# Parameter stage rebuilt: the left rows of x first, the matrices' angles by TensorE, 21 projection groups there, and table rounds without matrices

## The chip, the cores and the metric

The kernel runs on one core of a Trainium2 chip. The metric is the time of one execution on the device in microseconds (us), the median of three runs. The engines are TensorE (PE in the profile, with its weight loads as PEld), VectorE (DVE), ScalarE (ACT), GpSimd (POOL) and SyncE (SP, which only issues transfers here).

## The reference

Two independent parts, `a` (a recurrent attention with a memory) and `b` (an S4 convolution), cut to what is computed:

```python
def _A_ref(x, mem0, Wq, Wk, Wv, Wo, seg_len):     # x (1,2048,1024), 32 heads of 128, memory 8 rows, segments of 32
    for s in range(n_seg):                        # 64 segments, each needs the memory that the one before left
        h = concatenate([mem, x[:, s*32:(s+1)*32]])
        q, k, v = h @ Wq, h @ Wk, h @ Wv
        p = softmax(where(mask, q k^T * scale, -1e9))
        o = (p v) @ Wo
        mem = o[:, :8]; outs.append(o[:, 8:])

def _B_ref(u, A_re, A_im, B_re, B_im, C_re, C_im, log_dt, Dskip):    # u (1,2048,1024), 128 states a channel
    dt = exp(log_dt); logdA = dt * (A_re + 1j*A_im); dB = dt * (B_re + 1j*B_im)
    P = exp(logdA[:, :, None] * arange(2048))
    K = einsum('dn,dnl,dn->dl', C_re + 1j*C_im, P, dB).real
    y = irfft(rfft(u, 4096) * rfft(K, 4096))[:2048] + u * Dskip      # convolution along time
```

## The kernel before, in words

There are four stages, one behind the other, since each needs what the one before it made.

**Parameter stage** (0 to about 101 us). The matrices A, B, C of part b, 128 partitions by 1024 values each, are turned into modulus, angle and turn of each state (`modulus`, `turn`, `angle`), and each result is cut into two or three bf16 parts (`put3`) that are stored to `PB` in DRAM. `matrices` fills `MF`, the cosines and sines of the Fourier matrices in bf16: per pair of columns VectorE makes the angles (L774), ScalarE rounds (L776), VectorE subtracts (L769) and takes the absolute (L765), ScalarE takes two sines (L766, L770). `transposes` loads x in 16 blocks of 128 rows (L98), transposes each by 8 matmuls (L108), and ScalarE keeps the last 8 of each 32 rows in `xTl` and sends the other 24 to `VXd` in DRAM (L111, L112). These last 8 rows of a segment are called the left rows here: their keys, queries and values can be projected ahead of the recurrence. `projections` does that, in groups of 8 matmuls of 512 columns (L168); 10 groups run in this stage. A loop steps the generators in turn.

**Table rounds** (to about 415 us). Sixteen rounds make the powers P from the parts. The order of one round is the string `ORDER`, whose words stand in program order on each engine; a dash marks work of the round before. `X?p` are the two power matmuls of an e (L1131) into the PSUM tile `pa`, of which there is one; `E?` is the exponential of 648 columns that ScalarE takes from it (L1139); `X?t` is the phase matmul (L1125) and `n?` VectorE's copy of it; `S?` and `C?` are sines and cosines of 1824 columns on ScalarE, `b?` an absolute on VectorE, `gi?` and `gr?` its products, `K?` the matmuls that sum them. Exponentials and sines need different function tables, so each round holds two ACT_TABLE_LOADs, one at the first exponential (L1139) and one at the first sine (L1152). Between this stand side jobs: `P` a projection group (six a round), `U` a group of the spectra of u (L961), and `M` eight transposes of `MF` (L940), copied by VectorE and stored to `MId` in DRAM by GpSimd. The words `p?`, `A?`, `u?` and `m` copy the results of the side jobs out of PSUM. Each sine also issues one of 15 copies of 512 KB from weights (12 of them DRAM to DRAM), and the evictions of projections issue queued stores, among them 16 value rows `VXd<-PVd` of 256 KB.

**Pointwise stage** (b = 0 to 15, to about 655 us). For each b, `spectrum(b)` is 64 matmuls of 256 columns (L1101), `pointwise(b)` is ten VectorE operations of 1024 columns (L1265 to L1276), which write `Bt`. From b=4, two `inverse` groups of 32 matmuls each (L1324) follow each spectrum; they read `MI`, the transposed matrices, which SyncE loads from `MId` at b=0 to 3. spectrum(b+1) stands ahead of pointwise(b) in program order.

**Attention** (to the end). 64 segments, one after the other; TensorE works on the projections and waits for weights `wst` that are streamed from the copies `WD` in DRAM.

Of the kernel before, what the change touches and what calls it, by code (L numbers as in the profile page):

```python
# [74 lines left out]
class Ahead:  # L75
# [18 lines left out]
    def transposes(self, pool, ps, ident):  # L94
        nc = self.nc
        def load(b):
            xb = pool.tile([128, self.Dm], BF16, name="xb", tag="xb")
            nc.gpsimd.dma_start(out=xb[:], in_=self.x[b * 128:(b + 1) * 128, :])  # L98
            return xb
        xbs = [load(b) for b in range(3)]  # L100
        yield
        for b in range(self.S // 128):
            if b + 3 < self.S // 128:
                xbs.append(load(b + 3))
            xb = xbs[b]
            pt = ps.tile([128, self.KC, 4, self.SL], BF16, name="pt_x", tag="ptx")
            for kc in range(self.KC):
                nc.tensor.transpose(out=pt[:, kc, :, :].rearrange("p a b -> p (a b)"), in_=xb[:, kc * 128:(kc + 1) * 128], identity=ident[:])  # L108
            yield
            xst = pool.tile([128, 4, self.KC, self.XM], BF16, name="xst", tag="xst")  # L110
            nc.scalar.copy(out=xst[:].rearrange("p s k r -> p k s r"), in_=pt[:, :, :, 0:self.XM])  # L111
            nc.scalar.copy(out=self.xTl[:, :, 4 * b:4 * b + 4, :], in_=pt[:, :, :, self.XM:self.SL])  # L112
            nc.sync.dma_start(out=self.VXd[4 * b:4 * b + 4, :, 256:].rearrange("s p f -> p s f"), in_=xst[:].rearrange("p s k r -> p s (k r)"))
            yield

    def projections(self):
# [3 lines left out]
        slices = [(m, t, c) for m, t, cs in (("k", 0, (0, 8)), ("v", 0, (0, 4)), ("q", 0, (0, 8)), ("v", 0, (4, 8)), ("k", 1, (0, 8)), ("v", 1, (0, 4)),  # L120
                                             ("q", 1, (0, 8)), ("v", 1, (4, 8))) for c in range(*cs)]

        def load(i):
            m, t, c = slices[i]
            w = self.pool.tile([128, KC, 256], BF16, name="wsl", tag="wsl", bufs=4)
            nc.sync.dma_start(out=w[:], in_=self.src(m)[:, :, 2048 * t + 256 * c:2048 * t + 256 * c + 256].rearrange("k p f -> p k f"))
            return w
        ws = [load(0), load(1), load(2)]
        take, vals = yield
        late = []  # L130
# [1431 lines left out]
```

## Time and profile before

| what | value |
|---|---|
| median of 3 runs | 2026.26 us (2025.77 to 2030.95) |
| the profiled execution | 2021.33 us, its span 2019.6 us |
| busy: PE, PEld, DVE, ACT, POOL | 1835.2, 1154.4, 1437.1, 949.2, 440.1 us |
| parameter stage (windows 0 to 102): PE, DVE, ACT, POOL busy | 39.3, 84.9, 69.4, 19.1 us |
| Sin load of the first round, of the last round | 113.24, 414.87 us |
| first operation of pointwise(0) (L1265) | 429.87 us |
| spectrum(5) starts | 477.79 us |

All times below are of the profiled execution, counted from the start of its span. The profile gives the busy time of every engine in 40 slices of the span; the timeline of an engine lists its instructions in order of start, with the idle time just before one and what ended it in brackets; a windows row gives the busy time of each engine in a stretch, then the granted TensorE clock, the share of time that the 16 DMA engines were busy, and what they moved. The busy time of a matmul is modelled and can overlap its neighbour, so steps are read from start to start.

### The profile page before, as it was taken

How to read it: one execution, taken by the hardware profiler on the slowest of the kernel's cores; microseconds unless marked ns; L12 is line 12 of the kernel's file. 1: busy time of each engine (PE TensorE's matmuls, PEld its weight loads, DVE VectorE, ACT ScalarE, POOL GpSimd, SP SyncE). 2: the span in 40 equal slices, each digit the busy share in tenths (PEclk: the TensorE clock that was granted, in tenths of full speed). 3: DMA queues.
4: the chain of work that ended last, by engine and by line, in shares of the span. 5: the costliest groups of instructions: out<-in, count | busy, mean ns of one | idle time of the engine just before them, and what ended most of it. 6: DMA issues, size and time to landing. Idle time of an engine off the chain costs nothing.

```text
span 2019.6 us, 75101 instructions
## 1 busy us (share of the span) xinstructions
PE 1835.2 (91%) x32170; PEld 1154.4 (57%) x32198; DVE 1437.1 (71%) x3442; ACT 949.2 (47%) x1662; POOL 440.1 (22%) x864
## 2 busy tenths in 40 slices
PE   1699999778999789999999999999999999999998
PEld 1365766567888445555555555555555555555554
DVE  8879999999998356766667666666766666676650
ACT  4888898831333334344444434344444434344430
POOL 2135555547000011111111111111111111111120
PEclk9999999998999889999999999999999999999999
DMA  6788996868456999999999999999999999999991
GB/s 172 187 231 270 265 269 179 221 188 264 153 158 231 343 326 348 339 336 345 345 345 350 332 335 353 344 335 344 351 324 343 346 344 352 336 349 332 345 346 40
DMA packets 352630, 591.60 MB, mean 293 GB/s; under 512 B 111312, under 2 KB 229408, under 8 KB 350248
## 3 DMA queue, kind: packets, MB, share of 16 engines
q1 hardware_dynamic: 297452, 527.25, 77.2%
q10 hardware_dynamic: 44812, 28.26, 4.6%
q0 software_dynamic: 10032, 31.28, 4.4%
q8 instruction: 252, 4.13, 0.8%
q14 instruction: 82, 0.67, 0.1%
HBM read 531.12 MB, written 66.05 MB: 296 GB/s over the span
## 4 chain that ended last, share of the span: by engine, by line
PE 37%; DMA 23%; DVE 4%; issue 1%; ACT 1%; POOL 0%; SPq 0%; ACTq 0%; DVEq 0%; POOLq 0%
PE acc L375 21%; DMA wst<-WD_v 9%; PE pp L488 8%; DMA wst<-WD_o 7%; PE pe L625 3%; DMA wst<-WD_k 2%; PE tr L386 2%; DMA wst<-WD_q 2%; DMA arena<-PKd 2%; PE pv L460 1%; PE pv L456 1%; DVE arena L582 1%; PE sc L400 1%; DVE arena L441 1%; ACT arena L582 1%
## 5 line engine op out<-in xcount | busy, mean ns | idle before, releaser
L375 PEld LDWEIGHTS <-a_hT 128*32 128x32 bf16 x12352 | 326.4, 96 | 320.0 <-issue 60.9
L381 ACT CAST arena<-acc 128x512 bf16<-128x512 f32 x384 | 224.7, 585 | 396.2 <-PE acc L375 320.8
L375 PE MATMUL acc<-W,a_hT 128*32 128x512 bf16 x4608 | 354.1, 381 | 0.0
L488 PEld LDWEIGHTS <-arena 128*32 128x32 bf16 x8256 | 217.2, 97 | 86.8 <-issue 63.4
L375 PE MATMUL acc<-wst,a_hT 128*32 128x512 bf16 x2304 | 229.6, 382 | 29.3 <-DMA wst<-WD_v 22.0
L389 POOL COPY arena<-arena 128x128 bf16<-128x128 bf16 x128 | 37.4, 292 | 840.7 <-DMA arena<-PKd 315.6
L296 DVE TENSOR_SCALAR arena<-keep 128x256 int32<-128x256 int32 (+1 forms) x512 | 175.4, 394 | 29.5 <-PE acc L375 28.3
L375 PE MATMUL acc<-MF,a_hT 128*32 128x512 bf16 x2048 | 172.0, 382 | 0.0
L488 PE MATMUL pp<-W_o,arena 128*32 128x256 bf16 x4096 | 138.2, 275 | 5.0 <-DMA W_o<-in_A_Wo_dram 5.0
L168 PE MATMUL pro<-xTl,wsl 128*128 128x512 bf16 x490 | 113.0, 383 | 12.5 <-ACT xTl L112 6.6
L415 DVE TENSOR_REDUCE a_mx<-sc 128x4 f32<-128x160 f32 (+1 forms) x192 | 71.6, 373 | 73.6 <-PE sc L403 71.8
L419 ACT ACTIVATE sc<-sc 128x160 f32<-128x160 f32 (+1 forms) x192 | 63.9, 333 | 122.6 <-DVE sc L416 121.9
L1101 PEld LDWEIGHTS <-MF 128*128 128x128 bf16 x1024 | 102.5, 100 | 30.8 <-issue 8.2
L503 DVE COPY arena<-tr 128x512 bf16<-128x512 bf16 x64 | 27.2, 425 | 126.7 <-PE tr L386 126.7
L423 DVE TENSOR_REDUCE a_mx<-sc 128x4 f32<-128x160 f32 (+1 forms) x192 | 72.8, 379 | 55.3 <-ACT sc L419 54.9
L1101 PE MATMUL hps<-KT,MF 128*128 128x256 bf16 x720 | 94.2, 283 | 15.0 <-DVE x L1266 11.1
L1139 ACT ACTIVATE E<-pa 128x648 bf16<-128x648 f32 x128 | 90.9, 710 | 33.1 <-PE pa L1131 27.9
L1324 PE MATMUL yp<-Bt,MI 128*128 128x256 bf16 x680 | 102.8, 273 | 0.7 <-ACT yb L1339 0.7
L450 POOL TENSOR_TENSOR arena<-arena,a_BD 128x128 bf16<-128x128 bf16 x128 | 51.1, 399 | 234.0 <-DVE arena L433 221.5
L582 ACT CAST arena<-pp 128x128 bf16<-128x128 f32 x64 | 17.0, 265 | 163.2 <-DVE arena L582 163.2
L168 PEld LDWEIGHTS <-wsl 128*128 128x128 bf16 x512 | 50.5, 99 | 72.0 <-issue 16.2
L375 PE MATMUL acc<-W_v,a_hT 128*32 128x512 bf16 x1280 | 91.1, 378 | 0.0
(330 smaller groups left out, 3892.1 us busy)
## 6 DMA issues: line engine op xcount, KB each, us to landing
wst<-WD_v SPq DMA_DIRECT2D x256, 512.0 KB
wst<-WD_k SPq DMA_DIRECT2D x192, 512.0 KB
wst<-WD_o SPq DMA_DIRECT2D x192, 512.0 KB
wst<-WD_q SPq DMA_DIRECT2D x128, 512.0 KB
Ud<-ux POOLq DMA_DIRECT2D x16, 1024.0 KB, 5.9
uq<-Ud SPq DMA_DIRECT2D x32, 512.0 KB
wsl<-in_A_Wk_dram SPq DMA_DIRECT2D x16, 512.0 KB
wsl<-in_A_Wv_dram SPq DMA_DIRECT2D x16, 512.0 KB
```

The lines of the kernel that those rows point to most:

```text
L168: nc.tensor.matmul(a[:], lhsT=w[:, kc, 128 * j:128 * j + 128], rhs=xTl[:, kc, :, :].rearrange("p s k -> p (s k)"), start=(kc == 0), stop=( ...
L296: nc.vector.tensor_scalar(out=out.bitcast(I32), in0=in_.bitcast(I32), scalar1=0, scalar2=None, op0=ALU.bitwise_or)
L375: nc.tensor.matmul(a[32 * g:32 * g + 32, o_:o_ + rhs.shape[1]], lhsT=hT[:, kc, :], rhs=rhs, start=(kc == 0), stop=(kc == KC - 1), tile_pos ...
L381: nc.scalar.copy(out=q, in_=a[:])
L415: nc.vector.tensor_reduce(out=m_, in_=x, axis=AX.X, op=ALU.max)
L419: nc.scalar.activation(out=flat(sc, i), in_=flat(sc, i), func=ACT.Exp, scale=scale)
L423: nc.vector.tensor_reduce(out=m_, in_=x, axis=AX.X, op=ALU.add)
L488: nc.tensor.matmul(po[32 * qt:32 * qt + 32, o_:o_ + rhs.shape[1]], lhsT=oT[:, h % 4, (h % 16) // 4, :], rhs=rhs, start=False, stop=(h == 3 ...
L625: nc.tensor.matmul(pe[n][:], lhsT=left[2 * b + hi // 16][:, 128 * (hi % 16):128 * (hi % 16) + 128], rhs=wo[u][:, 1024 * hh + 512 * n:1024 ...
L1101: pe.matmul(s_[r][half][:, cs, :], lhsT=MF[:, kc, 4 * rr + mc, cs, :], rhs=rhs, start=(i == 0 and mc == 0), stop=(i == 1 and mc == 3), ski ...
L1139: sc.activation(out=T["E", r, e // 4][:, lo:lo + 8 * NE].rearrange("p (i c) -> p i c", i=2), in_=T.pop(("p", r, e))[:, :, 0:4 * NE], func= ...
L1324: pe.matmul(yp[:, b, :], lhsT=m_[:, b, cs, kc, :], rhs=Bt[:, kc, j, half, c_, :], start=(kc == 0 and cs == 0 and half == 0), stop=(kc == 3 ...
```

## The change

- **Left rows first.** Only the left rows of x are loaded in the parameter stage: four loads of 128 rows, 8 transposes each, four copies into `xTl`. The other 24 rows of each segment go through `other_rows` in the pointwise stage: 16 blocks of 96 rows, 8 transposes and a ScalarE copy each, 3 blocks at b=2, 7 at b=3 and 6 at the start of b=4. Two blocks share one tile; two such tiles are loaded at first, and the next pair is loaded when the second block of a pair is transposed.
- **Angles by TensorE.** `matrices` goes. Seven small rows on each side give the angle of every element of `MF` as a matmul with 7 contracted rows (32 matmuls of 128x512, words `F`), and ScalarE takes one sine of each from 16 bits of the PSUM values (words `f`). 24 small transposes and three copies prepare the rows.
- **Parameter algebra.** The reciprocal and the minimum and maximum are replaced by logarithm and exponential on ScalarE and some products on GpSimd; the loads are split between the queues of SyncE and ScalarE; the order of the whole stage is written out by hand in `PAR`.
- **Projections.** 21 groups run in the parameter stage (10 before), and five a round (six before). Weight slices are 512 columns wide in two tiles, and a group of the values is 8 matmuls of 512 columns (16 of 256 before).
- **Rounds.** No `M` and no trip through `MId`; a new `ORDER`; the exponential of an e is two instructions of 324 columns, one for each bank of `exps`.
- **Moved to the pointwise stage.** `matrices_back` at b=0, 1 and 2 (5, 6 and 5 times 8 transposes), copied by ScalarE straight into `MI`. The 15 copies and the 16 value rows are issued two and two a b from b=4.

```diff
-    def transposes(self, pool, ps, ident):
...
+    def other_rows(self, two, stage, bank, ident):
+        nc, n = self.nc, 4 * self.XM
+        x_s = self.x.rearrange("(s r) d -> s r d", r=self.SL)
+        blocks = list(range(self.NS // 4))
+        xbs = []
+
+        def load():
+            t_ = two()
+            for i in range(2):
+                b = blocks.pop(0)
+                xb = t_[0:n, 1024 * i:1024 * i + 1024]
+                nc.gpsimd.dma_start(out=xb, in_=x_s[4 * b:4 * b + 4, 0:self.XM, :])
+                xbs.append((b, xb))
+        load()
+        load()
         yield
+        while xbs:
+            b, xb = xbs.pop(0)
+            pt = bank()[:, :, 0:n]
             for kc in range(KC):
+                nc.tensor.transpose(out=pt[:, kc, :], in_=xb[:, 128 * kc:128 * kc + 128], identity=ident[0:n, 0:n])
+            xst = stage()
+            nc.scalar.copy(out=xst.rearrange("p s k r -> p k s r"), in_=pt.rearrange("p k (s r) -> p k s r", r=self.XM))
+            nc.sync.dma_start(out=self.VXd[4 * b:4 * b + 4, :, 256:].rearrange("s p f -> p s f"), in_=xst.rearrange("p s k r -> p s (k r)"))
+            if b % 2 and blocks:
+                load()
             yield
...
+        def matrix(i):
+            mt = take([128, 512], F32, "mf")
+            pe.matmul(mt[:], lhsT=turns_l[:, i // 2, :], rhs=turns_r[:, i % 2, :], start=True, stop=True)
+
+            def evict():
+                sc.activation(out=MF[:, :, i // 2, i % 2, :], in_=mt[:].bitcast(I16)[:, 0:1024:2].rearrange("p (k n) -> p k n", k=4), func=ACT.Sin,
+                              scale=float(TWO_PI / 65536))
+            return evict
...
+    exps = ps_e.tile([128, 2, 512], F32, name="pa", tag="pa")
...
     def power_matmuls(r, e):
         r, e = (r, e) if e else (r + 1, 0)
-        pa = T["p", r, e] = ps_e.tile([128, 2, 512], F32, name="pa", tag="pa")
         for i in range(2):
-            pe.matmul(pa[:, i, 0:4 * NE], lhsT=pars[r][:, e, :], rhs=RE[:, 4 * i:4 * i + 4, :].rearrange("p a b -> p (a b)"), start=True, stop=True)
+            pe.matmul(exps[:, i, 0:4 * NE], lhsT=pars[r][:, e, :], rhs=RE[:, 4 * i:4 * i + 4, :].rearrange("p a b -> p (a b)"), start=True, stop=True)
...
-        sc.activation(out=T["E", r, e // 4][:, lo:lo + 8 * NE].rearrange("p (i c) -> p i c", i=2), in_=T.pop(("p", r, e))[:, :, 0:4 * NE], func=ACT.Exp)
+        for i in range(2):
+            sc.activation(out=T["E", r, e // 4][:, lo + 4 * NE * i:lo + 4 * NE * i + 4 * NE], in_=exps[:, i, 0:4 * NE], func=ACT.Exp)
...
+    def matrices_back(n):
+        for _ in range(n):
+            c = turned_back.pop(0)
+            mt = ps_m.tile([128, 2, 4, 128], BF16, name="mt", tag="m")
+            for kc in range(4):
+                for cs in range(2):
+                    pe.transpose(out=mt[:, cs, kc, :], in_=MF[:, kc, c, cs, :], identity=ident[:])
+            sc.copy(out=MI[c // 2][:, c % 2], in_=mt[:])
...
+    held = bp.tile([128, 4, 2, 2, 2, DQ], BF16, name="xst", tag="B")[:].rearrange("p a b c d e -> p (a b c d e)")
...
     for b in range(16):
         dq = b // 4
+        if b == 4:
+            for _ in others:
+                pass
...
+        matrices_back((5, 6, 5)[b] if b < 3 else 0)
+        for _ in range({2: 3, 3: 7}.get(b, 0)):
+            next(others)
...
-        if b < 4:
-            for i in (2 * b, 2 * b + 1):
-                sy.dma_start(out=MI[i][:], in_=MId[2 * i:2 * i + 2].rearrange("c p a k q -> p c a k q"))
+        for _ in range(2 if b >= 4 else 0):
+            for jobs in (copies, ahead.after):
+                if jobs:
+                    jobs.pop(0)()
```

## The prediction

> **What bounds the kernel now.** I read the slices of the page first, then the timelines of ScalarE, TensorE and VectorE at the points where one stage hands over to the next, then busy time by windows. The two rows of slices below cut the span into 40 parts of 50.5 us.
>
> ```profile
> PE   1699999778999789999999999999999999999998
> ACT  4888898831333334344444434344444434344430
> ```
>
> Slices 1 and 2 (to 101 us) are the parameter stage, slices 3 to 9 the table rounds, 10 to 13 the pointwise stage, the rest attention. TensorE is idle only in the parameter stage and around the hand-over at 400 to 475. Attention is not touched. The rounds come next, as ScalarE ran one of them (start, duration, instruction, idle time before and releaser):
>
> ```profile
> 201.94 1.28 ACT L1139 ACT_TABLE_LOAD   x1 [0.40 <-DVE gr L1114]
> 203.24 0.71 ACT L1139 ACTIVATE E<-pa 128x648 bf16<-128x648 f32 x1
> 203.84 0.58 ACT L177 CAST kst<-pro 128x512 bf16<-128x512 f32 x1
> 204.47 0.71 ACT L1139 ACTIVATE E<-pa 128x648 bf16<-128x648 f32 x1
> ...
> 211.01 0.71 ACT L1139 ACTIVATE E<-pa 128x648 bf16<-128x648 f32 x1 [0.63 <-PE pa L1131]
> 212.25 0.71 ACT L1139 ACTIVATE E<-pa 128x648 bf16<-128x648 f32 x1 [0.53 <-PE pa L1131]
> 212.97 1.28 ACT L1152 ACT_TABLE_LOAD   x1
> ```
>
> The Sin load returns every 19.95 us: 11.03 from the Exp load to the Sin load, 8.9 from there to the next Exp load, which waits for VectorE's last product. In the 11.03, one exponential starts per 1.24 to 1.34 us: `pa` is one buffer, an exponential is .71, and the refill by two matmuls costs the .53 of the last rows. TensorE is nearly full there too (19.89 of 20 us), so either could set the period. The round of 381.47 tells: only two of its six projection groups are left and TensorE works 13.35 of 20 us, yet it lasts 19.95 to the next Exp load, as the others do.
>
> ```profile
> 381.47 1.28 ACT L1139 ACT_TABLE_LOAD   x1 [0.40 <-DVE gr L1114]
> 401.43 1.28 ACT L1139 ACT_TABLE_LOAD   x1 [0.87 <-DVE gr L1114]
> 414.87 1.28 ACT L1152 ACT_TABLE_LOAD   x1
> ```
>
> So the rounds are bound by the ring of ScalarE, `pa` and VectorE, and a projection group taken out of them frees nothing. Then TensorE at the hand-over to the second half of the pointwise stage:
>
> ```profile
> 468.28 6.62 PE L1101 MATMUL hps<-KT,MF 128*128 128x256 bf16 x36 [4.84 <-DVE x L1266]
> ...
> 477.79 4.09 PE L1101 MATMUL hps<-KT,MF 128*128 128x256 bf16 x36
> ...
> 484.78 7.15 PE L1324 MATMUL yp<-Bt,MI 128*128 128x256 bf16 x64
> 491.77 4.09 PE L1101 MATMUL hps<-KT,MF 128*128 128x256 bf16 x36
> ```
>
> spectrum(5) starts right behind spectrum(4); from there one b is 128 matmuls in 13.98 us (477.79 to 491.77), back to back; the windows show how little is spare (length, then busy time of PE, PEld, DVE, ACT and POOL, clock, DMA share, GB/s):
>
> ```profile
> 494.00:508.00 14.00, 14.00 (x131) 12.55 (x129) 13.21 (x15) 5.17 (x7) 11.47 (x19) 1.00 0.52 154
> 508.00:522.00 14.00, 14.00 (x130) 12.54 (x129) 13.25 (x15) 6.39 (x8) 0.57 (x2) 1.00 0.65 210
> ```
>
> **Parameter stage: -36.** It ends, before, with an Exp load at 100.59 and the first Sin load at 113.24. The matrices' work leaves VectorE: 16 scalings at .44 from start to start, 8 subtractions at 1.14 and 8 absolutes at .6 are 21 us. A reciprocal of 6.55 goes too. ScalarE loses 8 magnitude copies at 1.04 and 16 sines at 1.05 (25 us), and the 16 copies of x of .7 (11 us); it gets 32 sines of 128x512. Their nearest rows are the 512-wide copies, .48 to .56, so 17 us. Summed from such rows, ScalarE has 54 us of work after (8 table loads 10, sines 17, copies of parts 10, other activations 8, copies of left rows, transposed columns and projections 7, issues 2), VectorE 49, GpSimd 20. TensorE has 21 projection groups at 1.87 (39 us) and 32 small matmuls at about .24 (8 us). It can start the groups when parameters, left rows and the first slice are in: 3.5 MB at the 243 GB/s of the first 20 us is 14.4. Then it ends at 61.5 and is the last; an eviction and a table load follow, and the first exponential is at 63.5 if nothing waits on anything else. Before, the longest engine, VectorE, was busy 84.9 of 102 us. With all of that waste the first exponential would be near 75. I take 66, nearer the sum since an order written out by hand interleaves the four engines; bounds 60 and 75. The eight exponentials behind it took 11.36 us before (101.88 to 113.24): first Sin load at 77.5, 35.7 earlier.
>
> **Rounds: +.3 each, about +4.** The intention of the split is that one bank refills while the other is read. But both halves lie in one tile: in the built program TensorE's wait stands at the first matmul of a pair and is for the second exponential, and ScalarE's wait stands at the first exponential and is for the second matmul. So the ring stays as it is, with two instructions in it. A 256-wide ScalarE copy in the trace goes from start to start in .27 and the 648-wide exponential in .605 (203.24 to 203.84); between them a half of 324 is .33, the pair .66: +.05 a pair, +.4 a round. Bounds: -.36 a round, if the steps above 1.24 (seven took 9.01 us) all shrink to it now that TensorE has 5 groups and no matrices, and +2.8, if a half costs the .48 of a 512-wide copy. I take 20.25 us, near the linear end. TensorE's load falls by a projection group (1.87) and 8 transposes (.5), VectorE's by a copy of .6, neither on the ring. The copies and value rows that leave cost nothing there either, since DMA at a share of 1.03 (240 to 260) did not lengthen a round.
>
> The Trainium skill ("ScalarE: Activation LUTs", "What ACT_TABLE_LOAD costs") gives an ACTIVATE 186 ns and .833 ns an element, with some 93 ns of overlap back to back, so an estimate of .36 for a half and +.09 for a pair, against the +.05 of the rows. By that page the rounds would cost 5 us more than I sum; the trace's 648-wide step, .605, lies under the page's .63.
>
> Fourteen rounds of 20.25 behind 77.5, a last one of 22.7 (22.35 before, cold, plus .35), and 14.4 to pointwise(0) (15.0 from 414.87 to 429.87, less the matrices' copy of .6) give 398.1 for its start against 429.87: -31.8.
>
> **matrices_back at b=0 to 2: 0.** 16 times 8 transposes (.5 us) and a ScalarE copy of .95. VectorE binds there at 11.83 a b; TensorE has 3 to 5 us idle and ScalarE over half. Without that cover it would be 8 us.
>
> **The other rows of x: +22.** Sixteen blocks of 8 transposes (.5 us). Three lie in idle time at b=2; 13 stand in TensorE's order between spectrum(4) and spectrum(5), where the rows above show no gap. Their work alone is 6.5 us. But two pairs of blocks are in flight, and GpSimd issues the next pair only when a pair's second block is transposed: pairs 3, 5 and 7 make a chain of three hops. A hop is two issues (.55 each), a landing and the transposes. The x loads of before are the nearest row:
>
> ```profile
> L98 POOL DMA_DIRECT2D xb<-in_A_x_dram x16: 536/545/883, 5.5 to 61.5; - x16
> ```
>
> and landed in 3.6, 4.6 (median) or 6.5 us. With .2 to wake, 5.9 a hop, 17.7, then the last blocks and their own start, 2: spectrum(5) starts 20 us late. Behind such idle time 8 matmuls took 1.92 instead of .87 to 1.03 (404.36 and 408.75), and 36 took 6.62 instead of 4.09: +2 for the clock. Queued behind the waiting transposes is all of TensorE's work; pointwise(4) waits as well, since the stage tile of these blocks is the buffer it writes. Nothing is won back, TensorE being full to about 655. Bounds: 15 (3.6 a landing) and 30 (6.5, and the last pair behind eight KT loads on GpSimd's queue).
>
> **Copies and value rows at b=4 to 11: 0.** Two 512 KB copies and two 256 KB row sets a b, 1.57 MB, at 269 GB/s (240 to 260) 5.8 us, beside .55 of 14 us: the share becomes .96. The rounds ran at that share unharmed; what it costs if not is a rival.
>
> **Sum.** -31.8 + 22 = -9.8 on the profiled execution of 2021.33: 2011.5. The median of the runs, 2026.26, stands 4.9 above it: **2016.4**. 0.3% (6 us) is about what a measurement here can tell from no change.
>
> **Rivals.** (1) *The split works*: the refill of one bank runs under the other half. Then ScalarE's own work sets the round, 8.9 + 1.28 + 8 x .66 + 5 x .6 = 18.45; 14 x 1.8 less gives -35 in all, 1991. For: the two banks are separate matmuls. Against: the waits as built. (2) *The x loads cost little*, because the chain starts before spectrum(4) ends and landings take 3.6: +8 instead of +22, 2002. For: two pairs are loaded beforehand. Against: three hops remain. (3) *The parameter stage keeps its waste*: first exponential at 75, net -1, 2025. (4) *DMA takes over at b=4 to 11*, the slower side: loads of KT, u and inverses land late behind the copies. If half of the 5.8 us shows, 8 x 2.9 = +23, net +13, 2040; it turns the sum at 1.2 us a b. For: share .96, and attention waits for DMA at .96. Against: the rounds at 1.03. (5) *A half costs like a 512-wide copy*, .48: a pair +.35, 2.8 a round, net +28, 2055; it turns the sum at .13 a pair. Against: the .27 step at 256.
>
> **How the numbers follow.** Forecast .50 (its own range 2004 to 2029: faster .38, same .07, slower .05); (1) .13 and (2) .11, faster; (3) .06, same; (4) .12 and (5) .08, slower. Faster .62, same .13, slower .25. The range from 1990 to 2040 takes in (1) to (4) and the bounds of the x loads, and leaves out (5) and some of the edges.
>
> **What would show it.** First Sin load near 77.5; Sin loads 20.25 apart, with each pair of exponentials still waiting .5 for `pa`; pointwise(0) near 398; some 20 us between spectrum(4) and spectrum(5) in which TensorE waits for `xb`; then 13.98 a b. Sin loads 18.5 apart make it (1); longer b's with waits for DMA make it (4).

## The result, and the profile after

The changed kernel is slower: a median of 2165.1 us (2155.76 to 2167.22) against 2027.43 (2025.77 to 2030.95) for the kernel before on the same chip, a ratio of 1.0668 with a 95% interval of 1.0633 to 1.0702. The profiled execution took 2164.64 us, its span 2162.9, which is 143.3 more than the 2019.6 of before. The forecast was 2016.4, in a range of 1990 to 2040. The page of after, the rows that answer to those shown of before (here a slice is 54.1 us):

```profile
PE   8787888867259996999999999999999999999989
ACT  7577777764113241443444444444444434434430
PEclk9899899988579997999999999999999999999999
```

TensorE is now at work from the first slice on, so the parameter stage did become denser. But the rounds (slices 3 to 9) stand mostly at 8 tenths where they stood mostly at 9, and a hole of 2 and 5 tenths is in slices 11 and 12, with a lower granted clock. The timelines of ScalarE, VectorE and TensorE give the marks at which the stages hand over:

| step | before | after | measured | forecast |
|---|---|---|---|---|
| first Sin load | 113.24 | 102.02 | -11.2 | -35.7 |
| first to last Sin load, 15 rounds | 301.6 | 377.2 | +75.5 | +4.6 |
| last Sin load to pointwise(0) | 15.0 | 18.9 | +3.9 | -0.6 |
| pointwise(0) to spectrum(5) | 47.9 | 122.9 | +75.0 | +22 |
| spectrum(5) to the end | | | +0.2 | 0 |

They sum to 143.4, the difference of the spans but for rounding. Two places carry more than the whole loss, the start wins 11.2 back, and of the 3.9 us in the third row 2.8 arise in the last round's sines, of which ScalarE starts the second pair later. The first place is the round; ScalarE ran one so (start, duration, instruction, idle time before and releaser), and the last Sin load stands below it:

```profile
189.58 1.28 ACT L1138 ACT_TABLE_LOAD   x1 [2.36 <-DVE gr L1113]
190.88 0.77 ACT L1138 ACTIVATE E<-pa 128x324 bf16<-128x324 f32 x2
...
194.89 0.77 ACT L1138 ACTIVATE E<-pa 128x324 bf16<-128x324 f32 x2 [1.47 <-PE pa L1129]
...
202.56 1.28 ACT L1151 ACT_TABLE_LOAD   x1
...
214.38 1.28 ACT L1138 ACT_TABLE_LOAD   x1 [2.35 <-DVE gr L1113]
...
479.17 1.28 ACT L1151 ACT_TABLE_LOAD   x1
```

From Exp load to Sin load 12.98 us instead of 11.03, from there to the next Exp load 11.82 instead of 8.91, and ScalarE waits 2.35 for VectorE's last product where it waited .40. In the same stretch, VectorE and GpSimd:

```profile
205.97 1.84 DVE L1155 TENSOR_SCALAR nr<-nr 128x1824 int32<-128x1824 int32 x1
...
208.55 1.63 DVE L1155 TENSOR_SCALAR nr<-nr 128x1824 int32<-128x1824 int32 x1
210.10 1.64 DVE L1112 TENSOR_TENSOR gi<-E,sn 128x1824 bf16<-128x1824 bf16 x1
211.67 1.09 DVE L1113 TENSOR_TENSOR gi<-E,wn 128x768 bf16<-128x768 bf16 x1
```

```profile
206.80 5.52 POOL L980 TENSOR_TENSOR ux<-us 128x256 f32<-128x256 f32 x4
```

GpSimd's last four additions for the spectra of u ran from 206.80 to 212.3, beside VectorE's absolutes and products. In the kernel before, a round had the same instructions apart from each other: the additions ended at 213.5 and the first absolute began at 216.31, VectorE above, GpSimd below:

```profile
216.31 1.10 DVE L1158 TENSOR_SCALAR nr<-nr 128x1824 int32<-128x1824 int32 x1
...
218.66 1.12 DVE L1113 TENSOR_TENSOR gi<-E,sn 128x1824 bf16<-128x1824 bf16 x1
```

```profile
210.72 2.78 POOL L980 TENSOR_TENSOR ux<-us 128x256 f32<-128x256 f32 x4
```

1.10 became 1.84, and four additions of 2.78 became 5.52: each side runs slower. Not every pair of instructions does this: in the kernel before, the additions ran beside VectorE's copies of the phase matmuls out of PSUM, and these took 1.17 for two there and .62 for one elsewhere. The second place is the hand-over between spectrum(4) and spectrum(5), TensorE first, then GpSimd's loads:

```profile
547.86 0.84 PE L132 MATMUL yp<-b_ident,xb 96*128 96x96 bf16 x16
554.23 0.82 PE L132 MATMUL yp<-b_ident,xb 96*128 96x96 bf16 x8 [5.52 <-DMA xb<-in_A_x_dram]
565.53 0.82 PE L132 MATMUL yp<-b_ident,xb 96*128 96x96 bf16 x8 [10.49 <-DMA xb<-in_A_x_dram]
570.93 0.82 PE L132 MATMUL yp<-b_ident,xb 96*128 96x96 bf16 x8 [4.58 <-DMA xb<-in_A_x_dram]
...
620.93 6.48 PE L1100 MATMUL hps<-KT,MF 128*128 128x256 bf16 x36
```

```profile
565.82 0.68 POOL L123 DMA_DIRECT2D xb<-in_A_x_dram  x1 [4.35 <-issue]
571.19 0.65 POOL L123 DMA_DIRECT2D xb<-in_A_x_dram  x1 [4.68 <-issue]
576.52 0.65 POOL L123 DMA_DIRECT2D xb<-in_A_x_dram  x1 [4.68 <-issue]
```

spectrum(5) begins 73.1 us after spectrum(4) ends, where it followed at once, since each of the last eleven blocks of the other rows of x waits for its own load. The loads are issued some 5.3 us apart although GpSimd waits for nothing that the program has ("issue"). The view of waits has both places (us in total, times, longest):

```profile
PE yp L132 <- DMA xb<-in_A_x_dram: 63.4, 11, 10.5
PE ptt L1124 <- DVE nr L1146: 47.3, 15, 9.7
PE pa L1129 <- ACT E L1138: 33.3, 63, 1.1
```

From spectrum(5) on all is as it was: spectra still start 13.97 apart (637.29, 651.26), and the windows show TensorE and VectorE as full as before, with a DMA share of .81 to .90 instead of .52 and .65:

```profile
665.00:679.00 14.00, 14.00 (x131) 12.54 (x130) 13.25 (x15) 6.99 (x8) 0.00 (x0) 1.00 0.90 301
679.00:693.00 14.00, 14.00 (x131) 12.55 (x129) 13.18 (x15) 3.28 (x6) 0.00 (x0) 1.00 0.81 238
```

### The profile page after: what moved, and what is told of

It reads as the page before. It is cut to its first block, busy times and chain, and to the rows that moved or that the text cites. A ratio compares the mean times of both kernels' runs of the same rounds, so it can differ in the third digit from the quotient of the medians.

```text
span 2162.9 us, 74852 instructions
## 1 busy us (share of the span) xinstructions
PE 1894.8 (88%) x32030; PEld 1150.2 (53%) x32030; DVE 1458.1 (67%) x3399; ACT 965.4 (45%) x1793; POOL 469.1 (22%) x865
## 4 chain that ended last, share of the span: by engine, by line
PE 37%; DMA 20%; DVE 3%; ACT 1%; issue 1%; POOL 0%; SPq 0%; ACTq 0%; POOLq 0%; DVEq 0%
PE acc L397 21%; PE pp L510 8%; DMA wst<-WD_v 8%; DMA wst<-WD_o 7%; PE pe L647 3%; DMA wst<-WD_k 2%; PE tr L408 2%; DMA arena<-PKd 2%; PE pv L478 1%; PE pv L482 1%; DVE arena L604 1%; PE sc L422 1%; ACT arena L604 1%; DMA wst<-WD_q 1%; PE tro L610 1%
## 5 line engine op out<-in xcount | busy, mean ns | idle before, releaser
L397 PE MATMUL acc<-W,a_hT 128*32 128x512 bf16 x4608 | 364.5, 381 | 0.0
L190 PE MATMUL pro<-xTl,wsl 128*128 128x512 bf16 x512 | 121.4, 387 | 8.3 <-DMA wsl<-in_A_Wq_dram 3.9
L1138 ACT ACTIVATE E<-pa 128x324 bf16<-128x324 f32 x256 | 98.8, 438 | 61.7 <-PE pa L1129 58.6
L1146 DVE TENSOR_SCALAR nr<-ptt 128x456 f32<-128x456 int16 x128 | 78.8, 626 | 44.5 <-PE ptt L1124 42.9
L1129 PE MATMUL pa<-RE,pt 128*128 128x324 bf16 x256 | 64.8, 338 | 35.7 <-ACT E L1138 33.3
```

Source lines behind the costliest of these rows:

```text
L190: nc.tensor.matmul(a[:], lhsT=w[kc][:, 128 * j:128 * j + 128], rhs=xTl[:, kc, :, :].rearrange("p s k -> p (s k)"), start=(kc == 0), stop=( ...
L397: nc.tensor.matmul(a[32 * g:32 * g + 32, o_:o_ + rhs.shape[1]], lhsT=hT[:, kc, :], rhs=rhs, start=(kc == 0), stop=(kc == KC - 1), tile_pos ...
L1138: sc.activation(out=T["E", r, e // 4][:, lo + 4 * NE * i:lo + 4 * NE * i + 4 * NE], in_=exps[:, i, 0:4 * NE], func=ACT.Exp)
L1146: v.tensor_scalar(out=T["n", r, e // 4][:, lo:lo + 8 * NT], in0=T.pop(("t", r, e))[:, 0:8 * NT].bitcast(I16)[:, 0:16 * NT:2], scalar1=floa ...
```

## The experiments

Spans are of one profiled execution each, against 2162.9 for after and 2019.6 for before. The runs were on several chips, on which the kernel before took 2019.2 to 2028.6, and the stretch from spectrum(5) to the end, whose instructions no experiment changes, took 1536.6 to 1553.6. So differences of some 10 us are read at the marks inside the trace, not from the span.

**e1: the other rows' loads on SyncE's queue** (after, one line).

```diff
-                nc.gpsimd.dma_start(out=xb, in_=x_s[4 * b:4 * b + 4, 0:self.XM, :])
+                nc.sync.dma_start(out=xb, in_=x_s[4 * b:4 * b + 4, 0:self.XM, :])
```

> Changed kernel, but the 16 loads of the other rows of x are issued by SyncE instead of GpSimd; everything else as it is. In the changed kernel GpSimd issued these loads one at a time, 5.0 to 5.6 us apart, with no wait in the program between them, and spectrum(5) started 73 us after spectrum(4) had ended (547.9 to 620.9). Theory A (GpSimd's queue holds only one such load at a time; each block costs a whole landing of 5 us): two loads of a pair land together, the chain is three hops of some 6 us, spectrum(5) starts 18 to 28 us after spectrum(4), and the whole is 45 to 55 us shorter (span 2108 to 2118). Rival B (the landing itself, or the DMA engines, set the 5 us, whoever issues): the gap stays 65 to 75 us and the span within 8 us of 2163.

Span 2139.2. TensorE at the hand-over:

```profile
562.03 0.82 PE L132 MATMUL yp<-b_ident,xb 96*128 96x96 bf16 x8 [5.11 <-DMA xb<-in_A_x_dram]
564.02 0.82 PE L132 MATMUL yp<-b_ident,xb 96*128 96x96 bf16 x8 [1.17 <-DMA xb<-in_A_x_dram]
...
592.54 0.82 PE L132 MATMUL yp<-b_ident,xb 96*128 96x96 bf16 x8 [9.99 <-DMA xb<-in_A_x_dram]
```

Both loads of a pair are now issued within 1.5 us, and the second block waits 1.2 instead of 4.6: the pairs exist on this queue. So it was GpSimd's queue that passed one load at a time. The gap shrank from 73.1 to 40.9, but spectrum(4) started 6.5 us later and one pair stood behind nine KT loads of 10.1 us on SyncE, so 23.7 of 143 came back, half of what was expected. From its issue to the transposes that wait for it, a load took 5.2 to 9.4 us on this queue; on GpSimd's, landings at the hand-over took mostly 4.7 to 5.4 us.

**e4: one exponential for an e** (after, unsplit).

```diff
-        for i in range(2):
-            sc.activation(out=T["E", r, e // 4][:, lo + 4 * NE * i:lo + 4 * NE * i + 4 * NE], in_=exps[:, i, 0:4 * NE], func=ACT.Exp)
+        sc.activation(out=T["E", r, e // 4][:, lo:lo + 8 * NE].rearrange("p (i c) -> p i c", i=2), in_=exps[:, :, 0:4 * NE], func=ACT.Exp)
```

> Changed kernel with one exponential of 648 columns per e, as before, instead of two of 324. Theory A (both halves lie in one tile, so the split adds only its own .05 to .06 us to a ring that was there before): each step of the ring falls from 1.29 to 1.235, a round by .4 to .5, span shorter by 6 to 8 us (2155 to 2157). Rival B (the split lets banks refill under each other and helps): the span grows by 5 us or more. Rival C (the rounds are not bound by this ring): within 2 us.

Span 2151.2. The 15 rounds took 366.0 instead of 377.2, a mean of .75 less a round; sine phases were the same, 11.81. The step of the ring at the end of a round is 1.235 instead of 1.295, and the median round is 24.20 instead of 24.61. The rest of the mean stands in four rounds of 25.6 in after, for which e4 has 22.6 to 24.2. So the split costs some .4 a round, and it is a small part of the loss.

**e2 and e3: moving GpSimd's additions by program order.** In e2 (after) they are emitted at the next round's first exponential, in e3 (before) at the first sine. Both collect the additions in a list and emit them later. The call that emits them in e2 (in e3 its condition is `h == 0`, in the sine):

```diff
+        if e == 0:
+            while kept:
+                kept.pop(0)()
```

> Changed kernel, but the six GpSimd additions of a spectra group (L977 to L980, 5.3 us alone) are held back until the first exponential of the next round, so that they no longer run beside VectorE's absolutes and products in the sine phase. No other instruction moves. Sine phase (Sin load to Exp load) now 11.82 us against 8.91 before; round 24.6 to 26 against 19.95. Theory A (the additions and VectorE's operations stretch each other: absolute 1.11 to 1.84, imaginary product 1.64 instead of 1.11): the sine phase falls to 9.2 to 9.5 (the copy p4' stays ahead of the absolute, .4), the absolutes to 1.1, the rounds by 2.4 to 2.9 each and the span by 36 to 48 us; TensorE waits less and keeps a higher clock, which may give up to 1 us a round more. Rival B (the sine phase is longer because VectorE starts late, behind p4', or ScalarE's sines are slower): the phase stays above 11 and the span within 10 us.

> Kernel before, with one change: the six GpSimd additions are held back from their place behind the fourth exponential to the first sine, into the sine phase, where the changed kernel has them. Theory A (collision of GpSimd's additions with VectorE): the sine phase grows from 8.9 to 10.8 to 11.8 us, the absolutes from 1.11 to 1.6 to 1.9, each of 15 rounds by 1.9 to 2.9, span 2019.6 + 28 to + 45 = 2048 to 2065. Rival B (no collision; the longer sine phase of the changed kernel is from its own order): span within 6 us of 2019.6.

e2: 2189.6, and e3: 2021.9. Neither did what it was made for. GpSimd goes through its own list as soon as its data is there: in e3 the additions still ran at 210.01, in the exponential phase, and nothing changed, so e3 tells nothing. In e2 they fell behind the loads of the parameters, which wait for TensorE, and ran from 215.98 to 221.2 in one block. VectorE's first absolute beside them:

```profile
215.86 6.31 DVE L1168 TENSOR_SCALAR nr<-nr 128x1824 int32<-128x1824 int32 x1 [0.16 <-ACT sn L1164]
```

6.31 instead of 1.11: it waited for the whole block of six, while the additions took no longer than alone (2.77 for the last four). The sine phase became 13.8. That was not planned, but it speaks for a collision and against a mere lack of time.

**e7: the spectra's groups back where they were** (after, `ORDER` only: U1 behind K0', u0 behind X5p, u1 behind E5, and with them u3' behind n2).

```diff
-         "... E4 n2 n3 X5p E5 u3' X4t X5t n4 X6p K1' E6 X7p X6t u0 x0' n5 E7 U1 x1' X7t n6 n7 S0 u1 S1 P4'"
+         "... U1 E4 n2 u3' n3 X5p u0 E5 u1 X4t X5t n4 X6p K1' E6 X7p X6t x0' n5 E7 x1' X7t n6 n7 S0 S1 P4'"
```

> Changed kernel, but in the order of a round the last spectra group U1 and its evictions u0 and u1 stand earlier (U1 behind K0', u0 behind X5p, u1 behind E5; they stood at the end, at E7 and S0), so that GpSimd's six additions run in the exponential phase, as in the kernel before. Theory A (GpSimd's additions and VectorE's two-source and fast operations exclude each other): absolutes 1.1 (were 1.84 and 1.63), products 1.1, sine phase 9.0 to 9.5 instead of 11.82, rounds 2.4 to 2.8 shorter; TensorE idles less before the first exponential, so that its clock stays up: another .5 to 1.5 a round. Span 2163 less 36 to 60, 2103 to 2127. Rival B (the phase is long because p4' and the order of VectorE's work start the absolute late): sine phase above 11, span within 10 us of 2163. In the run with the additions merely issued later (behind the parameter loads) they ran from 215.98 to 221.2 and the absolute beside them took 6.31 us, which speaks for A.

Span 2112.9, 50 us less. A round as ScalarE ran it, and the absolute in it:

```profile
221.44 1.28 ACT L1138 ACT_TABLE_LOAD   x1 [0.87 <-DVE gr L1113]
...
233.22 1.28 ACT L1151 ACT_TABLE_LOAD   x1
```

```profile
236.27 1.11 DVE L1155 TENSOR_SCALAR nr<-nr 128x1824 int32<-128x1824 int32 x1 [0.88 <-ACT sn L1151]
```

The sine phase is 8.92 again and the absolute 1.11. The exponential phase fell too, from 12.98 to 11.78: with no long wait for VectorE ahead of it TensorE does not start cold. Its groups for u took 1.76 and 1.57 there in after and 1.03 in before; the clock over the rounds was .90 in after, .97 here, .98 in before. Most rounds are 20.69. Of the .74 above the 19.95 of before, .5 is one step of the ring: U1 now stands behind K0' and ahead of X5p, and ScalarE's exponential at 229.84 comes 1.82 after the one ahead of it, .57 of that in a wait for `pa`, where that step was 1.33. The rest, some .25, is what is left for the split. A few rounds are longer, the longest (26.77) with a wait of TensorE of 4.5 for a weight slice.

**e8: the collision made in the kernel before.** As e3, but the additions wait for the first sine by a copy of one column of it.

```diff
+                                if after_sine:
+                                    gp.tensor_copy(out=x_[:, 0, 0, 0:1], in_=after_sine.pop()[:, 0:1])
                                 gp.tensor_tensor(out=x_[:, 0], in0=e_[:, 0], in1=o_[:, 0], op=ALU.add)
```

> Kernel before, with the additions of GpSimd made to wait for the first sine of the round by a one-column copy that reads it; this time they really run in the sine phase (in the run that only issued them later nothing held GpSimd back, and they still ran at the fourth exponential). Theory A (collision): sine phase 10.8 to 14 us instead of 8.91, one absolute stretched to between 1.8 and 6.3, span 2019.6 + 28 to + 75. Rival B: sine phase 8.9 to 9.2, span within 6 us.

Span 2098.0, 78 us longer than before, a little beyond the range; the 15 rounds are 66.5 longer. VectorE and GpSimd in a round:

```profile
210.89 1.87 DVE L1174 TENSOR_SCALAR nr<-nr 128x1824 int32<-128x1824 int32 x1 [0.23 <-ACT sn L1162]
212.68 2.19 DVE L1123 TENSOR_TENSOR gi<-E,sn 128x1824 bf16<-128x1824 bf16 x1
```

```profile
213.85 5.18 POOL L986 TENSOR_TENSOR ux<-us 128x256 f32<-128x256 f32 x4
```

The sine phase is 12.34 instead of 8.91 and the rounds, but for the first, are 23.4 to 26.2. Some 48 of the 66.5 us are the sine phases; the rest is in the exponential phases, where TensorE's first groups for u take 1.91 instead of 1.03 behind a wait of 3.33. Nothing of the change is in this kernel except the time at which GpSimd adds, and issues what stands behind the additions in its list. With e7 the cause is shown from both sides.

**e5, e6: the parameter stage, one suspect each** (after). In e5 VectorE takes the four subtractions of GpSimd; in e6 the next slice is loaded one group earlier.

```diff
-        for k, x, eng in (("1", x1, gp), ("2", x2, v), ("6", x6, gp), ("4", x4, v), ("3", x3, v)):
+        for k, x, eng in (("1", x1, v), ("2", x2, v), ("6", x6, v), ("4", x4, v), ("3", x3, v)):
```

```diff
-                if j == 1 and 1 <= i < len(slices) - 1:
+                if j == 0 and 1 <= i < len(slices) - 1:
```

> Changed kernel, but the four subtractions by which two of the parameters are cut into parts are done by VectorE (1.22 us each) instead of GpSimd (2.4 to 3.1 us each). Theory A (GpSimd is on the path of the parameter stage, by its own time and by stretching VectorE beside it, 1.96 and 2.54 and 2.01 us for operations of 1.22 or less): the first exponential comes 4 to 8 us sooner than 83.05, first Sin load 94 to 98, span less by 4 to 8. Rival B (the stage is bound by TensorE's groups and their weights): the first exponential moves by less than 2, and VectorE's added 4.9 us make it later. Rival C: the first exponential is earlier, but the second still waits for the weights of a projection group (8.5 us in the changed kernel), so that the first Sin load stays at 101 to 103.

> Changed kernel, with the load of the next weight slice issued one projection group earlier (behind the first group of a slice, not the second). In the changed kernel SyncE issues loads and stores in one order: a slice of Wq is issued at 83.4, behind stores that wait for results, and lands for its group at 91.5, so that the second exponential waits 8.5 us, and every third round is 25.6 instead of 24.6 us. Theory A (the late slice is what the start of the rounds waits for): the second exponential follows the first within 4 us, first Sin load 95 to 99, rounds of 25.6 fall to 24.7; span 6 to 12 us shorter. Rival B (SyncE's stores block either way, or the buffers of the slice before are still read): within 3 us.

e5: 2156.8, first Sin load 100.86; e6: 2162.3, first Sin load 101.18. In after it is 102.02, so neither is the cause by itself. e5 brought the first exponential .6 us forward, and the second still waited 8.53. In e6 the waits for the slice fell from 2.56 and 1.30 to 1.01 and .54, and in their place came one of 4.06 for the next thing on SyncE's queue, `u_h`.

**e9 to e11: the other rows in the rounds.** e9 is after's parameter stage with a round order like that of before (five groups, the spectra early), one exponential for an e, and a block of the other rows, copied by VectorE, in the place of the matrices. The pointwise stage has no blocks left. e10 loads the next block right behind the transposes and has the early slices of e6; e11 has that load too, and before's slices of 256 columns.

```diff
-ORDER = ("p4' X0t' b0' w0' P2' b1' X1t gi0' C0' gr0' X0p' P0 P3 n0 P1' C1' E0 ... E7 U1 x1' X7t n6 n7 S0 u1 S1 P4'").split()
+ORDER = ("X0t' w0' X1t b0' C0' b1' P3' P1 X0p' gi0' P0 C1' gr0' p3' n0 P2 E0 ... x0' O' n5 X7t n6 E6 X7p P4' K1' u0 n7 p4' E7 x1' S0 m' S1").split()
```

> Changed kernel with three things put back: the order of a round as in the kernel before less its sixth projection group, with one block of the other rows of x (load, 8 transposes, VectorE copy, store) in the place of the eight transposes of the matrices; one exponential of 648 columns per e; nothing of the other rows in the pointwise stage. The parameter stage, 21 projection groups there, the wide slices, the matrices at b=0 to 2, copies and value rows at b=4 to 11 stay. Theory A (the loss is the collision in the sine phase, the cold clock behind it, and the serial loads; the rest of the change is sound): first Sin load near 101, rounds 19.95 to 20.3, last Sin load 402 to 407, spectrum(5) some 63 us behind it, so 465 to 472, and a span of 2006 to 2015, 5 to 14 us less than before. Rival B (five groups and no matrices leave TensorE so idle that the clock falls and rounds stay above 21.5): span above 2030.

> The run with the other rows in the rounds (span 2030.9), with two orders mended: the next block of rows is loaded right behind the transposes of the last (its load stood behind the eviction, and the last one came only at 427.4, which held pointwise(0) back to 440.1), and the next weight slice one group earlier, as in the run on slices. Theory: pointwise(0) 15 us behind the last Sin load instead of 25.9, so -11; rounds of 21.5 to 22.4 that waited for a slice fall to 20 to 20.5, -4 to -8. Span 2010 to 2018, less than the 2019.6 of before by 2 to 10. Rival: the slices wait for SyncE's order whatever the place of the load, then 2017 to 2022 from the first mend alone.

> As the run with the other rows in the rounds and their loads right behind the transposes, but with the weight slices of the kernel before (256 columns, four buffers, three slices ahead, 16 matmuls of 256 for a group of the values) instead of the wide ones of two halves; still 21 groups in the parameter stage and five a round. Theory A (the wide slices shorten the reach of the prefetch to one slice, so groups wait for weights at the hand-over and every third round): first Sin load 92 to 100 (105.9 with wide slices), rounds 19.95 to 20.2 throughout, span 1998 to 2010. Rival B (the weights wait for SyncE's order, not for buffers): first Sin load above 103 and span within 6 us of the run with early wide slices.

e9: 2030.9, e10: 2024.6, e11: 2029.2. Nearly all of the rounds' loss and all of the hand-over's is gone: of the 75.5 us in the rounds 6.7, 1.5 and 3.5 are left, with most rounds at 19.95 (e9 has three between 21.5 and 22.4, two of which wait for slices; e10 has one of 22.18), and it is 13.97 a b. spectrum(5) starts at 487.0, 482.2 and 485.0 (477.8 before), so none of the three gains yet. Most of what is left is behind the last round. pointwise(0) follows the last Sin load by 25.9 us in e9 and 26.8 in e10, where before had 15.0. The last block's load stood on GpSimd's queue behind the wait for a store, as GpSimd's timeline of e9 shows:

```profile
427.44 0.73 POOL L118 DMA_DIRECT2D xb<-in_A_x_dram  x1 [9.43 <-DMA Ud<-ux]
```

In e10 the first block's load did the same at the other end: it waited until 73.40 and held the loads of the parameters, so that the first exponential came at 91.6. e11's slices changed nothing (first Sin load 106.62, against 105.65 in e10).

**e12: the blocks one round earlier**, the first load behind the first parameters (e10, otherwise).

```diff
-         "... x0' O' n5 X7t ... x1' S0 m' S1"
+         "... x0' O n5 X7t ... x1' S0 m S1"
...
     ob = ahead.other_rows(tmp, take, ident)
-    next(ob)
...
     pars = {0: load_par(0)}
+    next(ob)
```

> The run with the other rows in the rounds and early slices (span 2024.6), with the first load of rows behind the first parameter loads on GpSimd's queue (it stood ahead of them, waited for its buffer until 73.4, and the first phase matmul came at 84.4), and every block one round earlier, so that none is left for the end (the last load was issued at 422.8 and spectrum(0)'s copies waited for its store). Theory: first Sin load 97 to 100 instead of 105.65; rounds 19.95; pointwise(0) 15 to 16 us behind the last Sin load instead of 26.8; together 17 to 19 us less, span 2005 to 2009, so 10 to 15 us (.5 to .75%) under the kernel before, and the changed kernel's sound parts are worth that much. Rival: the rounds' start is held by weights and u loads on SyncE's queue, first Sin load stays near 104, and the span 2011 to 2015. If the whole is above 2019 the parameter stage gained nothing.

Median 2014.55 us (2009.16 to 2024.97) against 2022.48 of before on its chip, ratio 0.9967 with an interval of 0.9949 to 0.9984: the rival's number, not the theory's. The profiled execution is the slowest of the eleven (span 2023.3), since its stretch from spectrum(5) to the end took 1553.6 where before's took 1541.8; up to there it is ahead. All rounds but the last are 19.95, pointwise(0) follows the last Sin load by 14.7, and spectrum(5) starts at 469.64 (477.79 before). The start of the rounds is what is left: the first Sin load is at 104.58, as the rival has it. ScalarE, two of the first eight exponentials:

```profile
92.94 0.71 ACT L1135 ACTIVATE E<-pa 128x648 bf16<-128x648 f32 x1 [8.35 <-PE pa L1127]
...
100.04 0.71 ACT L1135 ACTIVATE E<-pa 128x648 bf16<-128x648 f32 x1 [3.44 <-PE pa L1127]
```

TensorE reaches their matmuls late, since the groups ahead of them wait for a slice (3.44 and .91) and for `u_h` (2.22), both queued on SyncE behind the stores of projections.

**e13, e14: the loads of the hand-over on ScalarE's queue.** e13 is e12 with slices 6 and 7 and the first `u_h` loads issued by ScalarE. e14 moves also the phase rows (`rt`) behind the last part (`lo2`) in `PAR`.

```diff
-                nc.sync.dma_start(out=w[h][:], in_=...)
+                (nc.scalar if i in (6, 7) else nc.sync).dma_start(out=w[h][:], in_=...)
...
+            if word == "P17":
+                u_first.append(load_uq(0, sc))
```

```diff
-         "... s2 mi3 F20 F21 d14 f19 f20 lo3 rt P15 ... P16 lo4 F26 lo2 rp f25 f26 ..."
+         "... s2 mi3 F20 F21 d14 f19 f20 lo3 P15 ... P16 lo4 F26 lo2 rt rp f25 f26 ..."
```

> The run with all mends so far (first exponential 83.9, first Sin load 104.6), but the two weight slices of the hand-over and the first four loads of u are issued by ScalarE's queue instead of SyncE's, where they stand behind stores that wait for evictions and for eight earlier transfers. Theory A (the 9 us between the first and second exponential and the 3.4 before the fifth are loads queued behind stores): the second exponential within 3.5 us of the first, no wait for u, first Sin load 93 to 97. Rival B (the transfers themselves are late, DMA being full at 75 to 95): first Sin load above 101. Rival C (ScalarE, waiting for the buffers of its loads, is late itself): the first exponential moves past 86.

> As the run with the hand-over's loads on ScalarE's queue, and in the parameter stage's order the 18 small VectorE operations of the phase rows (rt, 57.7 to 62.7 in the changed kernel) stand behind the last part (lo2) instead of ahead of it. Theory A (the last part, its store, and the parameter loads behind it are what the first phase matmul waits for, and rt's 5 us lie in front of it): the last part is done 4 to 5 us sooner (66.9 before), and so are the first phase matmul (78.2) and the first exponential (83.9); first Sin load 88 to 93; span 12 to 18 us under the kernel before in the same call, ratio .991 to .994. Rival B (ScalarE's copies of parts wait for their buffers, not for VectorE): first exponential within 2 us of the run without this.

e13: span 2010.5, first Sin load 100.10 (104.58 in e12). The second exponential follows the first in 1.2 us, but the first comes 4.9 later than in e12, at 88.73, past the 86 of rival C, and three rounds are between 20.9 and 23.4. e14: span 2002.5, first Sin load 97.28 (88 to 93 expected); median 2004.54 us (2002.53 to 2005.9) against 2027.84 (2020.89 to 2030.24), a ratio of 0.9891 with an interval of 0.9864 to 0.9917. It is 1.1% faster than the kernel before, clear of the noise. ScalarE at its start:

```profile
85.23 1.28 ACT L1138 ACT_TABLE_LOAD   x1 [3.78 <-DMA xb<-in_A_x_dram]
86.52 0.71 ACT L1138 ACTIVATE E<-pa 128x648 bf16<-128x648 f32 x1
87.76 0.71 ACT L1138 ACTIVATE E<-pa 128x648 bf16<-128x648 f32 x1 [0.53 <-PE pa L1130]
...
97.28 1.28 ACT L1151 ACT_TABLE_LOAD   x1
```

The wait of 8.35 ahead of the second exponential is gone. The first comes no earlier than in e12 (83.88), though the last part is ready by 65.2 instead of 67.6 in e13: the first phase matmul (78.55) stands behind TensorE's projection groups, with no idle time between. The eight take 10.8 us instead of 20.7. Of the 17.1 us by which this span is shorter than before's, 16.0 stand at the first Sin load and stay to the end.

## Why the prediction was wrong, step by step

**Rounds, +4.6 forecast, +75.5 measured.** The step that failed is the one that kept the 8.9 us of the sine phase and put nothing of the side jobs "on the ring". It counted what left the round and did not follow what the new `ORDER` moves within it. The word `U1` had gone from the middle of the exponentials to behind the last, and `u1` behind `S0`; so GpSimd's additions, which need their result, ran beside VectorE's absolutes and products. GpSimd does not appear in its working on the rounds. The runs size it: 52.5 us of the 75.5 went with the words put back (e7, first to last Sin load), the cooled clock of TensorE among them. Of the 23.1 that e7 has above before, 11.1 are the .74 of every round, for U1's place and the split, and 12 are in a few longer rounds. e12 has none of the loss, with 301.9 for the 15 rounds, but which of its edits took which part was not tried apart.

The Trainium skill ("SBUF — State Buffer", "Who interferes with whom") says that VectorE and GpSimd share one pair of ports to the memory, and that where VectorE runs in a mode that takes this pair, whichever instruction issues first has it whole while the other stands still. The trace agrees for single instructions: the absolute grew by .73, and one 256-wide addition alone takes .70 (2.78 for four). In e2 the absolute lost to six additions in a row. That the ports are the reason is the word of the Trainium skill; the runs show only that the two engines stretch each other.

**The split.** The forecast that it brings no overlap was right: in after a pair with no other copy ahead of it still waits .53 for `pa`, and rival (1), 18.45 a round, did not come. Its price was right too: .05 a pair and .4 a round forecast, .06 for a step of the ring and .41 for the median round measured (e4). Rival (5), .35 a pair, is out. The estimate of .09 a pair from the Trainium skill ("ScalarE: Activation LUTs", "What ACT_TABLE_LOAD costs") is above the .06 of the trace, and the trace decides.

**Other rows, +22 forecast, +75.0 measured.** The mechanism was the forecast one: TensorE stands in its order and waits for `xb`, pointwise(4) behind it, and the clock drops. The landing was sized right as well; the view of the DMA queues has a median of 5.0 us for the 16 loads, against the 3.6 to 6.5 allowed:

```profile
xb<-in_A_x_dram POOLq DMA_DIRECT2D x16, 192.0 KB, 5.0
```

What failed is "two pairs of blocks are in flight": a pair was a pair in the program only. With one load at a time the chain has not three hops but eleven waits, 63.4 us in all, and the KT loads between them. (The .2 to wake in its hop stands in no row; in after the transposes began some .05 behind a landing.) The row of before could not show that: its 16 loads are spread over 56 us.

**Parameter stage, -36 forecast, -11.2 measured.** The first exponential came at 83.05 (101.88 before, 66 forecast), and the eight of the first round took 18.97 us instead of the 11.36 carried over. The step that failed is the sum by the busiest engine, first of all for that engine itself. TensorE was the last, as forecast, but it was to end its 21 groups at 61.5 and was through with them at 79.06, where the first phase matmul follows without idle time:

```profile
56.71 1.89 PE L190 MATMUL pro<-xTl,wsl 128*128 128x512 bf16 x8 [2.15 <-DVE kst L199]
...
63.43 0.58 PE L907 MATMUL mf<-mfw 7*128 7x512 bf16 x1 [4.08 <-DVE kst L199]
63.94 3.59 PE L178 MATMUL pro<-wsl,xTl 128*128 128x512 bf16 x8
...
79.06 0.36 PE L1124 MATMUL ptt<-RT,pt 128*128 128x456 bf16 x1
```

Of the 17.6 us, 4.9 are a later start (the first group at 19.33, not 14.4), 6.7 are waits, most of them for VectorE's copies of earlier groups (`kst`), and 5.9 are four groups that took 2.7 to 3.6 instead of 1.9, each the first or second behind idle time. The sum also has no term for the chain behind the last part, which goes through DRAM: part ready at 66.9, the four loads of the first parameters issued from 69.25 and landed by 77.66, 1.4 before that phase matmul, then power matmul 81.17 and exponential 83.05. So the two end almost together. In these 16 us TensorE is busy for 15.7 at a granted clock of .82, with a DMA share of 1.06. The part itself was late; some VectorE steps were stretched beside GpSimd's subtractions, though taking these away (e5) gained little: there the parameters landed 2.0 earlier, at 75.64, and the phase matmul came only .6 earlier, again right behind the 21st group (VectorE, then ScalarE, of after):

```profile
53.52 2.54 DVE L872 TENSOR_TENSOR x<-x,part 128x1024 f32<-128x1024 f32 x1
...
60.76 2.01 DVE L840 TENSOR_SCALAR RT<-RT,ang 128x456 bf16<-128x456 bf16 x1
```

```profile
81.76 1.28 ACT L1138 ACT_TABLE_LOAD   x1 [1.91 <-DMA PVd<-vst]
83.05 0.77 ACT L1138 ACTIVATE E<-pa 128x324 bf16<-128x324 f32 x2
...
92.81 0.77 ACT L1138 ACTIVATE E<-pa 128x324 bf16<-128x324 f32 x2 [8.51 <-PE pa L1129]
```

A subtraction of 1.22 took 2.54, a step of .34 took 2.01. The 8.51 is the queue: e13 and e14 took it away by moving loads from SyncE to ScalarE. Even there the first exponential is at 86.5, 21 us after the last part, with the phase matmul behind TensorE's groups as in after; a wait of 3.78 ahead of it is put down to a load of x, and what holds ScalarE there was not settled.

**What was right.** `matrices_back` at nothing: from pointwise(0) to the end of spectrum(4) is 49.8 us instead of 47.9, with the three blocks and a colder spectrum(4) in it. The copies and value rows at b=4 to 11 at nothing: 13.97 a b at a share of .9, so rival (4) is out. A projection group fewer freed nothing: e12's rounds of five groups take the 19.95 of before. Rival (3), the waste that stays in the parameter stage, was right in kind, and (2) went the wrong way. No rival had a time beyond 2055.

## What to carry to other kernels

When an order is rewritten, follow each moved word to the engines that run behind it, and lay their new times beside the instructions of every other engine there, also where an engine is far from full: six additions a round, which began 6.5 us later against the Sin load than before, were worth some 50 us. Count transfers as in flight only where the trace shows two of that size and queue in flight. For a stage that fills a pipeline, give the busiest engine's sum a term for its waits and for the slow instructions behind them, and sum the chain behind the last input (store, load, matmul, table) beside it.

## What the hardware showed that was not expected

- GpSimd and VectorE slow each other by whole instructions: 1.11 to 1.84 and 2.78 to 5.52 where they alternate, 1.11 to 6.31 where GpSimd ran six additions without a gap.
- GpSimd's queue passed one load of 96 rows of 2 KB at a time, mostly 5.0 to 5.6 us apart, each issue some .3 behind the landing of the load before, with nothing awaited in the program; of the four loads of 128 rows at the start of after, three were issued at once and the fourth 4.29 us behind the third. SyncE's queue issued two loads of 96 rows in 1.47 us. What holds GpSimd's back was not settled.
- A wait of TensorE of 2.65 us for VectorE and one of 1.07 for ScalarE were followed by groups of 1.76 and 1.57 us that take 1.03 otherwise, so an idle stretch at one end of a round is paid for again in the next.
